# One region of program order for the opening and the first pass of a gated MLP, and five moves within it

## The chip, the cores and the metric

The kernel runs on one core of a Trainium2 chip. Its engines work side by side and meet through semaphores: TensorE (PE, with the load of its stationary operand listed apart as PEld), VectorE (DVE), ScalarE (ACT), GpSimd (POOL) and SyncE (SP), which issues all transfers. Each engine takes its instructions from a queue in order. The metric is the device time of one execution in microseconds. Before the change the median of 3 runs is 545.57 us (545.38 to 546.04).

## The reference

x is 2048 x 1024, w_gate and w_up are 1024 x 3584, w_down is 3584 x 1024, all bf16:

```python
g = jnp.einsum("bsd,df->bsf", x, w_gate)
u = jnp.einsum("bsd,df->bsf", x, w_up)
h = gelu(g) * u                      # tanh form
return jnp.einsum("bsf,fd->bsd", h, w_down)
```

## The kernel before

**Products by Winograd's scheme.** A matrix product split 2 x 2 needs eight half-size products; the kernel uses the form with seven, at the price of sums of operands. For the first two products the halves are: the two groups of 512 rows of x (c = 0, 1), the two halves of the 1024 input columns (k < 4 and k >= 4 in steps of 128), and a pair of 128-wide blocks of the weights. The sums of x are called T1 to T4, those of the weights S1 to S4 (`sums_t`, L148, `sums_s`, L163); TB and SA are plain casts of one quarter each to the type that PE wants. The T sums are made once by VectorE. The S sums are made by GpSimd for each pair of weight blocks while PE works on the pair before; only the first set is made by VectorE. The casts TB and SA are made by ScalarE.

**Passes and units.** There are two passes (`ip`) over 1024 rows each. A pass has 14 units (`unit`, L221), each for two of the 28 weight blocks, gate and up; then `down` multiplies the 1024 rows of h by w_down with the same scheme. A unit has 40 matmuls in five pairs of four: (S2, T2) accumulated onto the block's first product P1 in the banks e; (S1, T1) into the banks d; (S3, T3) onto e; (S4, TB) onto d; (SA, T4) onto e. Between them ScalarE copies e away as U2 (L108, before S3's product comes on top) and d as P5 (before S4's product comes on top), VectorE adds and multiplies, and ScalarE makes the gelus (L193). Gate and up have a bank each, so each of these steps is two instructions. In the first pass the copies U2 and P5 go to spare memory of the second half of x (`spare0`, listed as xT).

**Opening.** The first eight blocks are treated apart, as blocks 0 to 7 of plain products (`early_p1`, `early_p2`, L515 to L527): their first product P1 = (first half of x's columns) x (first half of the weights' rows) is copied away (`early_snap`, one of gate and up into a place of hT, the other into a slot p), the second product is added, and `early_c11` (L534) makes a gelu and a multiplication of the sum. These blocks' saved P1 come back later: unit u (u < 8) takes block u as its first and block u + 8 as its second block, and needs block u's P1 in its banks e. `seed` (L537) is the put-back, two copies by ScalarE. Unit 0's is made in the opening, that of unit u + 1 at the end of unit u (`ahead_of_p4`), in front of the fifth pair of products.

Before the first products, x's first 512 rows are turned by PE against an identity (`turn`, L456, four quarters) and copied out of PSUM; the other 512 rows are turned on their way in by SyncE's transposing transfers (L485), whose second half carries the operand of T2's and TB's inputs.

**Preparing w_down.** From unit 2 on the first pass also makes, for one 128-row block j of w_down per unit, three differences m for the last product (`keep_part`, L271): ScalarE casts a piece of the raw block into an idle PSUM bank (L277), VectorE subtracts. The first cast stands before U2 (`keep(0, ...)`), the second and third behind it. Then SyncE stores the differences (`store_made`, L287, 768 KB) and behind that fetches the raw block of the next unit (`fetch_wd`, L258, two loads of 256 KB, L269).

**Order.** SP, DVE, POOL and PE issue in the order of the source throughout. ScalarE does so only inside two kinds of region: one around the opening (L541), one around the units of each pass (L612). Within a region ScalarE keeps the order of the source; how the instructions of two regions fall between one another is left to the scheduler. `down` lies outside. Buffers of 2 KB per partition come from a pool of 52 slots (`slot`, L83), reused as they come free; weights have three larger ones.

Of the kernel before, what the change touches and what calls it, by code (L numbers as in the profile page):

```python
# [10 lines left out]
def kernel(  # L11
# [24 lines left out]
    ENG = mybir.EngineType  # L36
# [23 lines left out]
    R = 8  # L60
# [26 lines left out]
    bank = [psum.tile([P, N], f32, name=f"bank{i}") for i in range(8)]  # L87
# [18 lines left out]
    def snap(ps, name, at=None):  # L106
        t = slot([P, N], f32, name) if at is None else at
        nc.scalar.copy(out=t, in_=ps)  # L108
        return t
# [76 lines left out]
    def make_s(w, eng):  # L186
        s = sums_s(w, eng)
        s.make("s1", "s2", "s3", "sa", "s4")
        return s
# [28 lines left out]
        g, up = add(c, p1)  # L218
        times(fb, 0, gelu(g), up)

    def unit(fbs, banks, s, t, spare, after_p5, aside, keep, ahead_of_p4, behind_p4):  # L221
        GU = range(2)
        e, c, d = banks
        for i in GU:
            product(e[i], s["s2"][i], t["t2"], False)
        aside()
        keep(0, c[0])
        u2 = [snap(e[i], "u2", spare[i]) for i in GU]
        keep(1, c[0])
        keep(2, c[1])  # L230
        up = c[1]
        c = d
        for i in GU:
            product(c[i], s["s1"][i], t["t1"], True)
        p5 = [snap(c[i], "p5", spare[2 + i]) for i in GU]
        after_p5()
        for i in GU:
            product(e[i], s["s3"][i], t["t3"], False)
        g = new(dve, e[0], p5[0], ADD, "sum", dtype=f32)
        dve(up, e[1], p5[1], ADD)  # L240
        for i in GU:
            product(c[i], s["s4"][i], t["tb"], False)
        times(fbs[1], 1, gelu(g), up)
        g, up = add(c, u2)
        times(fbs[0], 1, gelu(g), up)
        ahead_of_p4()
        for i in GU:
            product(e[i], s["sa"][i], t["t4"], False)
        behind_p4()
        times(fbs[1], 0, gelu(e[0]), e[1])  # L250
# [108 lines left out]
    sa = {}  # L359
# [96 lines left out]
    def turn(ps, half, a, parts):  # L456
        tp = ps.bitcast(bf16).rearrange("p (k r) -> p k r", k=KH)
        for t in range(2):
            for k in range(KH):
                nc.tensor.transpose(  # L460
                    tp[:, k, t * P : (t + 1) * P], xn[half, a][:, t, k * P : (k + 1) * P], ident
                )
        n = KH // len(parts)
        for m, put in enumerate(parts):
            ks = slice(m * n, (m + 1) * n)
            put(  # L466
                out=xT[0][:, half * KH : (half + 1) * KH, a * 2 * P : (a + 1) * 2 * P][:, ks],
                in_=tp[:, ks],
            )
# [35 lines left out]
    def early(u):  # L505
        if u // 2 not in pairs_of:
            pairs_of[u // 2] = load_w((R + u) // 2, new_w())
        return [first[u], block_of(pairs_of[u // 2], u % 2)]
# [25 lines left out]
    def early_c11(u, ps):  # L534
        times(block(0, u, 0), 0, gelu(ps[0]), ps[1])

    def seed(u, e):  # L537
        for i in range(2):
            nc.scalar.copy(out=e[i], in_=p1s[u][i])

    with tc.manual_schedule(engines={ENG.Activation}):  # L541
        for _ in range(NWARM):
            nc.tensor.matmul(bank[3], lhsT=warm[:, :P], rhs=warm, start=True, stop=True)
        turn(bank[4], 0, 0, (on_dve,))
        turn(bank[5], 0, 1, (on_dve, on_act))
        pairs = [(u, ps, i) for u, ps in ((0, E), (1, K)) for i in range(2)]
        for cols in (slice(0, 2 * P), slice(2 * P, N)):
            for u, ps, i in pairs:
                early_p1(u, ps, i, range(0, 2), cols)
        for u, ps, i in pairs[:2]:  # L550
            early_p1(u, ps, i, range(2, KH))
        early_snap(0, E)
        turn(bank[6], 1, 0, (on_dve,))
        early_p1(*pairs[2], range(2, KH))
        turn(bank[7], 1, 1, (on_dve,))
        early_p1(*pairs[3], range(2, KH))
        early_snap(1, K)
        for ks in (range(0, 2), range(2, KH)):
            for u, ps, i in pairs:
                early_p2(u, ps, i, ks)  # L560
        early_c11(0, E)
        early_c11(1, K)
        four = ((2, C), (3, F), (4, E), (5, K))
        for u, ps in four:
            for i in range(2):
                early_p1(u, ps, i, range(KH))
            early_snap(u, ps)
        t.make("t1", "t2")
        for u, ps in four:
            for i in range(2):  # L570
                early_p2(u, ps, i, range(KH))
            early_c11(u, ps)
            if u == 3:
                t.make("t3")
            if u == 4:
                t.make("t4")
        seed(0, F)
        two = ((6, E), (7, K))
        for u, ps in two:
            for i in range(2):  # L580
                early_p1(u, ps, i, range(KH))
            early_snap(u, ps)
        t.make("tb")
        s.make("s1", "s2")
        pool_behind(s["s2"][-1][:, 0])
        s.make("s3", "s4", "sa")
        for u, ps in two:
            for i in range(2):
                early_p2(u, ps, i, range(KH))
            early_c11(u, ps)  # L590
        nxt = {"s": make_s(early(1), pool)}
    spare0 = [as_f32(xT[1][:, 2 * m : 2 * m + 2]) for m in range(4)]

    def making(u):
        if u < 2 or u >= NU:
            return []
        return list(range(u - 2, NJ if u == NU - 1 else u - 1))
# [13 lines left out]
    for ip in range(NPASS):  # L611
        with tc.manual_schedule(engines={ENG.Activation}):  # L612
            if ip == 0:
                ws = {}
            else:
                raw_of(0, F)()
                raw_of(1, C)()
            for u in range(NU):
                js = making(u) if ip == 0 else []

                def prepare():
                    if "s" not in nxt and u + 1 < NU:
                        nxt["s"] = make_s(weights(ip, u + 1), pool)
                    if len(js) == 1:
                        store_made(js[0])
                    for j in js[1:]:
                        keep_whole(j)
                    if ip == 0:
                        fetch_wd(making(u + 1))

                def keep(part, ps):
                    if js:
                        keep_part(js[0], part, ps)

                def aside():
                    if u + 2 < NU:
                        weights(ip, u + 2)

                def ahead_of_p4():
                    if u % 2 and u + 1 < NU and (ip or u + 1 >= R):  # L640
                        raw_of(u + 1, F)()
                        nxt["c11"] = raw_of(u + 2, C)

                    if ip == 0 and u + 1 < R:
                        seed(u + 1, F if u % 2 else C)

                def behind_p4():
                    if "c11" in nxt:
                        nxt.pop("c11")()

                if u % 2 and (ip or u):
                    E, K, C = C, E, K
                banks = (E, K, C) if u % 2 else (F, K, E)
                unit(
                    [block(ip, u, h) for h in range(2)], banks, s, t,
                    [None] * 4 if ip else spare0,
                    prepare, aside, keep, ahead_of_p4, behind_p4,
                )
                s = nxt.pop("s", None)

        last = ip == NPASS - 1
        got, nxt = {}, {}

        def more(step):
            if last:
                return
            if step in (-1, 0, 2):
                store_made({-1: NJ - 3, 0: NJ - 2, 2: NJ - 1}[step])
            if step == 0:
                xT[:] = new_x()  # L670
            if step >= 24 and step % 2 == 0 and step // 2 - 12 < len(moves):
                c, ko = moves[step // 2 - 12]
                transposing(xT, c, ko, (2 * (ip + 1) + c) * N)
            if step == 50:
                ws.clear()
                loaded(0), loaded(1)
            if step == 58:
                got["s"] = make_s(loaded(0), dve)
            if step == 62:
                got["t"] = make_t(xT)  # L680

        down(ip, F + K, C + E, last, more)
        E, K, C, F = K, E, F, C
        if not last:
            t, s = got["t"], got["s"]
# [29 lines left out]
```

## Time and profile before

| what | value |
|---|---|
| median of 3 runs | 545.57 us |
| the profiled execution: its time | 544.05 us |
| its span, first to last instruction | 542.3 us |
| PE busy | 534.3 us (99%) |
| DVE, ACT, POOL busy | 336.5, 273.3, 246.1 us |
| granted PE clock | 1.00 throughout |
| end of opening on PE, start of unit 0 | 36.0 us |
| start of units 1, 2, 3 on PE | 47.85, 57.10, 66.35 us |

A line of a timeline holds the start and the length in us from the span's start, the engine, the line of the kernel, the operation, what it writes and reads by the program's names, the shapes, how many instructions were merged, and in brackets how long the engine had been idle and what ended that. A line number may be that of a helper: L115 is every plain matmul, L91 every VectorE operation on two tensors, L94 the same of GpSimd, L103 a cast, L108 a copy out of PSUM, L193 a gelu, L539 a put-back of P1. "SPq" is SyncE's queue with its transfers. Matmuls are pipelined: starts are exact, ends modelled.

### The profile page before, as it was taken

What the parts mean: (1) busy time and instruction counts of PE and PEld (TensorE: products, weight loads), DVE (VectorE), ACT (ScalarE), POOL (GpSimd) and SP (SyncE); (2) the same over time, 40 slices, a digit from 0 to 9 for tenths busy, and PEclk for the clock granted to TensorE, in tenths of its full rate; (3) what the DMA queues carried; (4) which work ended last, traced back from release to release, by engine and by line L of the source; (5) the groups of instructions that cost most, each with busy time, mean ns of one, the idle gap of its engine ahead of it and who ended that gap; (6) DMA issues with size and microseconds to landing.
All of it is one profiled execution on the core that took longest, in us unless ns stands there. A gap on an engine that the chain in (4) does not pass through costs nothing.

```text
span 542.3 us, 7464 instructions
## 1 busy us (share of the span) xinstructions
PE 534.3 (99%) x2399; PEld 383.2 (71%) x2399; DVE 336.5 (62%) x516; ACT 273.3 (50%) x487; POOL 246.1 (45%) x221
## 2 busy tenths in 40 slices
PE   8979999999999999999999999999999999999997
PEld 4438787868676745888868676776768685488885
DVE  1675777667676795594964564555554639676730
ACT  4566787857666410166346555555555551114431
POOL 0049999986873500000076767676766600000000
PEclk9999999999999999999999999999999999999999
DMA  8943366956481999989854222232521049563751
GB/s 241 260 119 111 105 181 190 250 175 216 134 255 50 355 388 342 249 213 253 302 158 114 77 79 77 79 105 58 145 59 24 0 136 390 192 233 97 232 186 50
DMA packets 106471, 93.29 MB, mean 172 GB/s; under 512 B 17088, under 2 KB 91840, under 8 KB 106432
## 3 DMA queue, kind: packets, MB, share of 16 engines
q1 hardware_dynamic: 106432, 92.82, 58.1%
q8 instruction: 19, 0.31, 0.2%
q14 instruction: 20, 0.16, 0.1%
HBM read 74.45 MB, written 15.20 MB: 165 GB/s over the span
## 4 chain that ended last, share of the span: by engine, by line
PE 93%; SPq 3%; DVE 2%; DMA 1%; ACT 1%; issue 0%; DVEq 0%
PE bank L115 93%; DVE t L91 1%; DMA xT<-in_x_dram 1%; SPq L127 1%; SPq L485 1%; DVE hT L91 0%; SPq L449 0%; ACT sa L103 0%; ACT xT L108 0%; ACT st L418 0%; ACT g L193 0%; DVEq L91 0%
## 5 line engine op out<-in xcount | busy, mean ns | idle before, releaser
L94 POOL TENSOR_TENSOR s<-w 128x512 fp32r<-128x512 bf16 x92 | 106.5, 1177 | 138.2 <-PE bank L115 100.5
L115 PE MATMUL bank<-t,s 128*128 128x512 f32 x672 | 158.4, 391 | 2.2 <-ACT g L193 2.2
L115 PEld LDWEIGHTS bank<-t,s 128*128 128x128 f32 x672 | 125.5, 188 | 30.8 <-ACT g L193 2.6
L91 DVE TENSOR_TENSOR hT<-g,bank 128x512 bf16<-128x512 f32 x112 | 76.9, 688 | 26.0 <-ACT g L193 15.4
L193 ACT ACTIVATE g<-sum 128x512 f32<-128x512 f32 x76 | 48.2, 634 | 70.1 <-DVE sum L91 66.9
L115 PE MATMUL bank<-xT,w 128*128 128x512 bf16 (+1 forms) x360 | 78.6, 375 | 0.7 <-DVE xT L466 0.7
L108 ACT COPY p<-bank 128x512 f32<-128x512 f32 x92 | 52.7, 589 | 45.3 <-PE bank L115 45.3
L91 DVE TENSOR_TENSOR sum<-bank,p 128x512 f32<-128x512 f32 x34 | 23.5, 692 | 75.9 <-PE bank L115 75.9
L115 PEld LDWEIGHTS <-w 128*128 128x128 bf16 x360 | 34.1, 98 | 41.7 <-issue 2.6
L115 PE MATMUL bank<-q 128*128 128x512 f32 x240 | 58.9, 389 | 0.0
L115 PEld LDWEIGHTS <-hT 128*128 128x128 bf16 x320 | 31.1, 98 | 38.9 <-issue 1.7
L115 PE MATMUL bank<-t,sa 128*128 128x512 f32 x224 | 57.2, 397 | 0.0
L115 PE MATMUL bank<-tb,s 128*128 128x512 f32 x224 | 55.3, 389 | 0.0
L115 PEld LDWEIGHTS bank<-q 128*128 128x128 f32 x240 | 45.1, 188 | 9.3
L103 ACT CAST tb<-raw 128x512 fp32r<-128x512 bf16 x28 | 17.3, 627 | 62.9 <-PE bank L115 29.9
L115 PEld LDWEIGHTS bank<-t,sa 128*128 128x128 f32 x224 | 42.1, 188 | 9.5
L115 PE MATMUL bank<-raw,hT 128*128 128x512 bf16 x224 | 48.7, 379 | 0.0
L115 PEld LDWEIGHTS bank<-tb,s 128*128 128x128 f32 x224 | 42.1, 188 | 8.7
L94 POOL TENSOR_TENSOR s<-w,s 128x512 fp32r<-128x512 bf16 x40 | 46.0, 1171 | 0.0
L94 POOL TENSOR_TENSOR s<-s,w 128x512 fp32r<-128x512 f32 x40 | 45.7, 1163 | 0.0
L91 DVE TENSOR_TENSOR q<-hT 128x512 fp32r<-128x512 bf16 x56 | 38.4, 686 | 3.6 <-PE bank L115 3.4
L108 ACT COPY xT<-bank 128x512 f32<-128x512 f32 x56 | 31.7, 590 | 10.2 <-PE bank L115 8.6
(54 smaller groups left out, 568.1 us busy)
## 6 DMA issues: line engine op xcount, KB each, us to landing
raw<-in_w_down_dram SPq DMA_DIRECT2D x76, 256.0 KB, 4.8
q<-td SPq DMA_DIRECT2D x60, 256.0 KB, 5.0
w<-in_w_gate_dram SPq DMA_DIRECT2D x24, 512.0 KB, 5.5
w<-in_w_up_dram SPq DMA_DIRECT2D x24, 512.0 KB, 6.6
td<-m SPq DMA_DIRECT2D x12, 768.0 KB, 4.5
w<-td SPq DMA_DIRECT2D x6, 1024.0 KB, 10.1
out_dram<-st SPq DMA_DIRECT2D x32, 128.0 KB, 1.8
hT<-in_w_gate_dram SPq DMA_DIRECT2D x3, 512.0 KB, 5.0
```

The lines of the kernel that those rows point to most:

```text
L91: nc.vector.tensor_tensor(out=out, in0=a, in1=b, op=op)
L94: nc.gpsimd.tensor_tensor(out=out, in0=a, in1=b, op=op)
L103: nc.scalar.copy(out=t, in_=src)
L108: nc.scalar.copy(out=t, in_=ps)
L115: nc.tensor.matmul(ps, lhsT=lhs, rhs=rhs, start=start, stop=stop, skip_group_check=True)
L127: nc.sync.dma_start(out=w[:, i, k0:k1], in_=src[k0 * P : k1 * P, f0 : f0 + wide * P].rearrange("(ko ki) f -> ki ko f", ki=P),)
L193: nc.scalar.activation(g, src, ACT.Gelu_apprx_tanh)
L485: nc.sync.dma_start_transpose(out=xT[1][:, half * KH : (half + 1) * KH], in_=x2[N : 2 * N, half * N : (half + 1) * N],)
```

## The change

- The opening becomes a function, `opening()`, called inside the first pass's region, so that ScalarE has one region of source order for both.
- The copy of the last turned quarter of x is split into two halves on VectorE.
- The four casts TB are made behind block 2's gelu instead of behind the copies of block 7's P1.
- T4 is made behind block 5's multiplication instead of behind block 4's.
- The two casts SA of unit 0 are made behind the last two early gelus instead of in front of them in the source.
- The put-back for unit u + 1 is made right behind U2 of unit u, not in front of its fifth pair of products.

```diff
-    def unit(fbs, banks, s, t, spare, after_p5, aside, keep, ahead_of_p4, behind_p4):
+    def unit(fbs, banks, s, t, spare, behind_u2, after_p5, aside, keep, ahead_of_p4, behind_p4):
...
         u2 = [snap(e[i], "u2", spare[i]) for i in GU]
+        behind_u2()
         keep(1, c[0])
         keep(2, c[1])
...
-    with tc.manual_schedule(engines={ENG.Activation}):
+    def opening():
...
-        turn(bank[7], 1, 1, (on_dve,))
+        turn(bank[7], 1, 1, (on_dve, on_dve))
...
             early_c11(u, ps)
+            if u == 2:
+                t.make("tb")
             if u == 3:
                 t.make("t3")
-            if u == 4:
-                t.make("t4")
+        t.make("t4")
         seed(0, F)
...
-        t.make("tb")
         s.make("s1", "s2")
         pool_behind(s["s2"][-1][:, 0])
-        s.make("s3", "s4", "sa")
+        s.make("s3", "s4")
         for u, ps in two:
             for i in range(2):
                 early_p2(u, ps, i, range(KH))
             early_c11(u, ps)
-        nxt = {"s": make_s(early(1), pool)}
+        s.make("sa")
+        return {"s": make_s(early(1), pool)}
...
             if ip == 0:
                 ws = {}
+                nxt = opening()
...
+                def behind_u2():
+                    if ip == 0 and u + 1 < R:
+                        seed(u + 1, F if u % 2 else C)
...
-                    if ip == 0 and u + 1 < R:
-                        seed(u + 1, F if u % 2 else C)
```

More of the change, by code (lines that the diff above doesn't have):

```diff
@@ L656 @@
                     [None] * 4 if ip else spare0,
-                    prepare, aside, keep, ahead_of_p4, behind_p4,
+                    behind_u2, prepare, aside, keep, ahead_of_p4, behind_p4,
                 )
```

## The prediction

> **What bounds the kernel now.** The page's first part comes first: TensorE (PE) is busy 99% of the span, every other engine at most 62%.
>
> ```profile
> PE 534.3 (99%) x2399; PEld 383.2 (71%) x2399; DVE 336.5 (62%) x516; ACT 273.3 (50%) x487; POOL 246.1 (45%) x221
> ```
>
> So an edit can win only where PE stands still or starts a product late. The timeline of PE alone names two such places in the first 45 us, both in the stretch that the change reorders:
>
> ```profile
> 31.89 4.48 PE L115 MATMUL bank<-xT,hT 128*128 128x512 bf16 x20 [0.88 <-DVE hT L91]
> 36.02 2.21 PE L115 MATMUL bank<-t,s 128*128 128x512 f32 x8
> 40.44 3.92 PE L115 MATMUL bank<-t,s 128*128 128x512 f32 x16 [2.21 <-ACT g L193]
> ```
>
> The 2.21 us is the wait of unit 0's second pair of products for the gelus of blocks 6 and 7. ScalarE's timeline shows why. The first half of block 6's sums is complete after 8 of the 20 matmuls from 31.89 on (0.216 apart, the last 0.38 long: 33.8), that of block 7 after 16 (35.5); but the two gelus (L193) stand behind unit 0's copies of U2 (L108) and two casts, although the source writes them first.
>
> ```profile
> 37.34 0.59 ACT L108 COPY xT<-bank 128x512 f32<-128x512 f32 x1 [1.72 <-PE bank L115]
> 38.27 0.59 ACT L108 COPY xT<-bank 128x512 f32<-128x512 f32 x1 [0.34 <-PE bank L115]
> 38.75 1.14 ACT L103 CAST sa<-w 128x512 fp32r<-128x512 bf16 x2
> 39.79 1.09 ACT L193 ACTIVATE g<-bank 128x512 f32<-128x512 f32 x2
> ```
>
> A third loss is spread out. All engines' timeline at a unit boundary (unit 3 starts at 66.35):
>
> ```profile
> 65.63 0.58 ACT L539 COPY bank<-hT 128x512 f32<-128x512 f32 x1
> 66.15 0.58 ACT L539 COPY bank<-p 128x512 f32<-128x512 f32 x1
> 66.32 0.76 PEld L115 LDWEIGHTS bank<-t,s 128*128 128x128 f32 x4 [0.31 <-POOL s L94]
> 66.35 0.94 PE L115 MATMUL bank<-t,s 128*128 128x512 f32 x3
> ```
>
> The seed copy (L539) into the first bank ends at 66.21; the weight load, 0.31 idle, starts 0.11 later (its releaser is listed as POOL, long done; it was the seed). In units 1 to 7 PE starts 0.14 after that copy each time. Last, what can bind once PE is sooner: ScalarE, VectorE and SyncE around unit 3 and 4.
>
> ```profile
> 69.64 1.49 DVE L91 TENSOR_TENSOR m<-bank,m 128x512 fp32r<-128x512 f32 x2 [1.06 <-ACT bank L277]
> ```
> ```profile
> 71.15 0.33 SPq L288 DMA_DIRECT2D td<-m  x1
> 71.57 1.33 SPq L269 DMA_DIRECT2D raw<-in_w_down_dram  x2
> ```
> ```profile
> 76.42 0.59 ACT L277 CAST bank<-raw 128x512 f32<-128x512 bf16 x1
> 76.93 0.59 ACT L108 COPY xT<-bank 128x512 f32<-128x512 f32 x1
> ```
>
> Read as a ring: the third difference m ends at 71.13, its store and then the raw loads of the next block are issued, the first raw lands 4.8 us after its issue (76.38), and ScalarE's first cast of unit 4 starts 0.04 later. This ring turns in 9.25 us, the length of a unit; PE is not held by it yet.
>
> **The change part by part.** Times are in the profiled execution (span 542.3, its own time 544.05); the median of the runs shown is 545.57, 1.5 more, and a saving is taken to be the same in both.
>
> *Copy of the last turned quarter in two halves.* PE waits 0.44 us until 11.00 for a 0.69 us copy begun at 10.16. A 128x512 copy out of PSUM took 0.42 (at 5.42), so the first half is there at 10.58 and PE could start 0.28 earlier. Its third matmul needs weights that land at 11.13 (issued 5.33, 5.8 us to landing). Between 0 and 0.28 I take 0.15. The extra instruction costs VectorE 0.15, in 3 us of idle time.
>
> *The four TB casts moved up, behind the gelu of block 2.* Their 0.52 us steps (2.18 for four) now stand before the gelu of block 3: gelu 2 at 22.27, casts to 24.94, gelu 3 at 24.84 for 24.14. The operand landed at 22.04, so they don't wait. VectorE multiplies block 3 at 25.48 for 25.15, and everything behind is 0.33 later: T3, product of block 4 ending 29.16 for 28.84.
>
> *T4 behind the multiplication of block 5.* That one now ends at 29.76 instead of 31.84. PE: the second half of block 6's first product writes the bank that block 4's multiplication reads; it starts at 29.21 instead of a free 28.97 (0.24 lost). The second half of block 7's starts at 30.94 instead of 31.89. The 0.88 wait is gone, 0.95 is gained so far. VectorE goes on to T4, until 32.17, to S2, until 34.58, and S4, until 36.99; PE needs S2 at 35.25, T4 not before 42. GpSimd's set for unit 1 starts 0.33 later (34.64) and has its S2 at 41.5; unit 1 starts at 44.4. Its sets take 9.02 us each, so it stays 3 us ahead. On SyncE's queue nothing changes place here: the weights of these units are issued by 28 us, before and after.
>
> *Gelus 6 and 7 before U2.* Gelu 6 can run at 32.85, gelu 7 at 34.6. Unit 0's second pair then waits for the first multiplication behind S4 (37.59), and for its own turn: 35.25 + 1.86 = 37.11 for the first bank, 38.03 for the second, 0.3 after it is free. That pair's start moves from 40.44 to 37.11; and the first matmul after the stall, 0.34 before the second one, falls back to 0.23. So 3.44 up to here. The casts of SA moved between (four, 2.1) push the U2 copies to 37.17 and 37.65, seeds to 38.14, P5 to 39.17 and 39.65: needed at 38.95, 39.85, 40.78 and 41.69. If the covering slack of 0.3 on the multiplication fails, the loss is what it is late; bounds 0 and 0.9, I take 0.
>
> *Seeds behind U2.* PE's undisturbed step in this stretch is 0.2267 us (second half of every unit), so 40 matmuls take 9.07. Units 1 to 6 start on PE at 47.85, 57.10, 66.35, 75.62, 84.89, 94.14, the seventh at 103.41: 55.56 for 54.41. With the ends, seven boundaries cost 1.29. The seeds now run 6 us earlier; nothing else ends last there (S2 is 3 us early). Between 0 and 1.29 I take all of it.
>
> *What the seeds are moved in front of.* Two copies at 0.517 us now stand between U2 and the second and third cast of the w_down differences (L277), from unit 2 to unit 6. Behind them wait the differences on VectorE, their store, and on SyncE's queue behind the store the raw loads of the next block; and the P5 copies, which free the bank of PE's fourth pair. With K the start of the first cast, T the unit's start, and ScalarE never idle, from the steps of the rows (cast 0.52, copy 0.49, seeds 0.48 and 0.52, casts 0.52 and 0.52, P5 0.52 + 0.59): the second cast is at K + 2.52, P5's first copy ends at K + 4.15, the third difference at K + 2.52 + 2.12 (69.01 to 71.13) = K + 4.64. The fourth pair wants P5 at T + 5.44, 0.14 ahead as with the seeds: PE is held when K > T + 1.15, by that excess and 0.12 of restart. From the end of the third difference to the next first cast the five rows have 4.82, 5.26, 4.81, 5.29, 5.27 (more where two weight loads follow), and 0.04. So the ring needs 9.5 or 9.95 us, against 9.07 for PE.
> Unit 2 has its raw early: K = T - 0.2; U2's second copy waits for PE until T + 2.06, so P5 is out at T + 5.21 (0.1 to spare, no stall) and the third difference at T + 5.69. Unit 3: K = T + 5.69 + 4.82 + 0.04 - 9.07 = T + 1.48, stall 0.45. Unit 4: K = T + 1.48 + 9.94 - 9.52 = T + 1.9, stall 0.9. Units 5 and 6 likewise 0.45 and 0.9. Unit 7 has no seed, so its P5 comes a microsecond sooner after K. Sum 2.7. Bounds: 0 if the raw loads come without the ring; upward, 0.8 more per landing gives 5.9.
>
> [...] The trace, whose stores of m take 3.9 to 5.5 us (median 4.5) to landing, decides for the long ring.
>
> Sum: -3.44 - 1.29 + 2.7 = -2.0, that is 542.0 in a profiled execution and **543.5** against the median. Later stages hold no idle PE and move along; the order on ScalarE from unit 8 on stays.
>
> **The rivals.** *Ring hidden (540.8).* If the raws land as early in the unit as now, all 4.7 us stay. For it: seeds leave the unit's end, which frees a buffer slot 6 us earlier. Against: VectorE's differences wait for L277 in 14 of 36 places, 15.9 us in all.
> *Ring a little longer (546).* The raw buffers are reused slots; where the first raw waits for the unit's first gelu (as the second raw at 62.80 does), its landing slips by some 0.6 in each of four units: 2.4 back, -2.0 + 2.4 = +0.4, no change that shows.
> *Slower (548).* The first raw waits for the unit's second gelu, as the very first raws do (issue held at 47.16 by an ACT gelu, landed 49.84, 2.7 later). That gelu ends 8.2 after K, the ring becomes 10.9, and units 3 to 6 stall 1.2 + 3 x 1.8, unit 7 0.7: -4.7 + 7.3 = +2.6. It decides from 0.8 us more per landing than the rows have.
> *The order isn't what costs.* If ScalarE's gelus were late for their inputs, nothing would move (545.6). Against: the gelu at 39.79 shows no wait at all.
>
> **How the numbers follow.** Computed ring 0.50 (its own range 542.3 to 544.4); hidden ring 0.15; a little longer, or no effect, 0.17; slower 0.18. A measurement of this kernel tells 0.2% (1.1 us) from no change. Faster 0.65, same 0.17, slower 0.18. The range starts at the hidden ring with the whole 0.28 of the split copy (540.7), takes in the longer ring at 546 and goes 0.8 into the way to the slower case: 546.8, which leaves out most of that case and little else.
>
> **What would show it.** Right: no idle PE before unit 0's second pair (about 37.1); units 1 and 2 of 9.07 us; PE waiting for ACT xT (P5) by 0.4 to 0.9 before the fourth pair (tb) of units 3 to 6; the first cast of these units 1.4 to 2 us after the unit's start, behind its raw load. Wrong: units 3 to 6 of 9.07 us (hidden), or of 10 to 11 us (slower); PE idle by hT L91 near 38 us; any PE wait after unit 8, for which I see no reason.

## The result, and the profile after

| | before | after |
|---|---|---|
| median of 6 runs each, us | 545.48 (544.79 to 546.04) | 542.84 (542.59 to 544.01) |
| the profiled execution: its time, us | 544.05 | 542.84 |
| its span, us | 542.27 | 541.03 |
| start of unit 1 on PE, us | 47.85 | 44.15 |
| start of unit 8 on PE, us | 119.55 | 118.30 |
| from unit 8 to the end, us | 422.72 | 422.73 |

The changed kernel takes 0.9958 of the time before (95% interval 0.9945 to 0.9972): faster, by 2.64 us between the medians. Between the two profiled executions it is only 1.24 us of span. Both figures matter below.

The page after, the busy times and the group of the fourth pair of products:

```profile
PE 534.3 (99%) x2399; PEld 383.6 (71%) x2399; DVE 335.4 (62%) x517; ACT 272.3 (50%) x487; POOL 246.3 (46%) x221
...
L115 PE MATMUL bank<-tb,s 128*128 128x512 f32 x224 | 55.7, 391 | 2.3 <-ACT xT L108 2.3
```

PE's busy time is what it was; the split copy shows as one instruction more on VectorE. New is the idle time in front of the fourth pair, ended by P5's copy on ScalarE (line numbers are one or so higher than before). First the opening, PE's timeline after:

```profile
14.09 21.11 PE L115 MATMUL bank<-xT,hT 128*128 128x512 bf16 x96
34.84 5.84 PE L115 MATMUL bank<-t,s 128*128 128x512 f32 x24
```

The 96 matmuls of the early blocks are in one piece, but for 0.23 us lost at 28.99 (see below), and so are unit 0's first three pairs: neither the 0.88 us wait in front of block 7's second half nor the 2.21 us in front of unit 0's second pair is left. ScalarE's timeline shows the gelus of blocks 6 and 7 ahead of the casts and copies:

```profile
32.64 0.60 ACT L193 ACTIVATE g<-bank 128x512 f32<-128x512 f32 x1 [0.28 <-PE bank L115]
34.37 0.60 ACT L193 ACTIVATE g<-bank 128x512 f32<-128x512 f32 x1 [1.13 <-PE bank L115]
34.86 2.17 ACT L103 CAST sa<-w 128x512 fp32r<-128x512 bf16 x4
36.93 1.07 ACT L108 COPY xT<-bank 128x512 f32<-128x512 f32 x2
```

Then the first units, PE's timeline again:

```profile
62.30 5.60 PE L115 MATMUL bank<-t,s 128*128 128x512 f32 x24
68.06 2.08 PE L115 MATMUL bank<-tb,s 128*128 128x512 f32 x8 [0.16 <-ACT xT L108]
...
77.97 2.06 PE L115 MATMUL bank<-tb,s 128*128 128x512 f32 x8 [0.56 <-ACT xT L108]
...
88.56 2.06 PE L115 MATMUL bank<-tb,s 128*128 128x512 f32 x8 [0.96 <-ACT xT L108]
...
98.53 2.08 PE L115 MATMUL bank<-tb,s 128*128 128x512 f32 x8 [0.65 <-ACT xT L108]
```

Units 3, 4, 5 and 6 each wait for P5. ScalarE's timeline gives the reason: the first cast of the raw w_down block waits for its load each time, and the casts, put-backs (L540) and copies queued behind it slip with it.

```profile
63.76 0.59 ACT L278 CAST bank<-raw 128x512 f32<-128x512 bf16 x1 [0.75 <-DMA raw<-in_w_down_dram]
...
73.67 0.59 ACT L278 CAST bank<-raw 128x512 f32<-128x512 bf16 x1 [1.23 <-DMA raw<-in_w_down_dram]
...
84.27 0.59 ACT L278 CAST bank<-raw 128x512 f32<-128x512 bf16 x1 [1.85 <-DMA raw<-in_w_down_dram]
84.79 1.07 ACT L108 COPY xT<-bank 128x512 f32<-128x512 f32 x2
85.75 0.60 ACT L540 COPY bank<-hT 128x512 f32<-128x512 f32 x1
86.27 0.60 ACT L540 COPY bank<-p 128x512 f32<-128x512 f32 x1
86.79 1.12 ACT L278 CAST bank<-raw 128x512 f32<-128x512 bf16 x2
87.83 1.08 ACT L108 COPY xT<-bank 128x512 f32<-128x512 f32 x2
...
94.23 0.59 ACT L278 CAST bank<-raw 128x512 f32<-128x512 bf16 x1 [1.28 <-DMA raw<-in_w_down_dram]
```

In unit 5 (it starts at 81.68) ScalarE stands idle for 1.85 us until the raw block lands; the first P5 copy then ends near 88.4, and PE starts its fourth pair at 88.56 after its longest wait. A bracket counts from the modelled end of the matmul before; counted from start to start, a wait loses some 0.2 to 0.3 us more, so that the 2.3 us of the page stand for a larger loss in the next table.

The start of each unit on PE, taken from the matmuls' starts, in us, and the length of the unit:

| unit | before, start | length | after, start | length | first cast after the start |
|---|---|---|---|---|---|
| 0 | 36.02 | 11.82 | 34.84 | 9.30 | |
| 1 | 47.85 | 9.25 | 44.15 | 9.07 | |
| 2 | 57.10 | 9.25 | 53.22 | 9.09 | -0.18 |
| 3 | 66.35 | 9.27 | 62.30 | 9.51 | 1.46 |
| 4 | 75.62 | 9.27 | 71.81 | 9.87 | 1.86 |
| 5 | 84.89 | 9.25 | 81.68 | 10.60 | 2.59 |
| 6 | 94.14 | 9.27 | 92.28 | 10.00 | 1.95 |
| 7 | 103.41 | 16.14 | 102.28 | 16.02 | 1.88 |

So the account between the two profiles is: 3.70 us gained up to unit 1, 2.46 us given back from unit 1 to unit 8 (74.16 for 71.70), nothing behind. Of the 3.70, some 0.36 lies ahead of block 2's first product (14.09 for 14.45): about 0.17 of it is the split copy. From the last matmul ahead of that copy's wait to block 2's first product pass 4.11 us for 4.28 (4.01 to 4.21 in the five profiles on record with the split, 4.27 to 4.28 in the five without). The other 0.19 lies ahead of that and is not the change's: block 2's first product starts between 14.09 and 14.98 over all ten profiles, in no order of kernels.

### The profile page after: what moved, and what is told of

Same layout as the page of the kernel before. It is cut to its first block, busy times and chain, and to the rows that moved or that the text cites. A ratio compares the mean times of both kernels' runs of the same rounds, so it can differ in the third digit from the quotient of the medians.

```text
span 541.0 us, 7444 instructions
## 1 busy us (share of the span) xinstructions
PE 534.3 (99%) x2399; PEld 383.6 (71%) x2399; DVE 335.4 (62%) x517; ACT 272.3 (50%) x487; POOL 246.3 (46%) x221
## 4 chain that ended last, share of the span: by engine, by line
PE 94%; ACT 3%; DMA 1%; DVE 1%; issue 1%; SPq 0%; ACTq 0%; DVEq 0%
PE bank L115 93%; DMA raw<-in_w_down_dram 1%; ACT xT L108 1%; ACT bank L540 1%; ACT bank L278 1%; PE bank L544 1%; PE bank L461 0%; DVE t L91 0%; ACT tb L103 0%; DVE m L91 0%; DVE hT L91 0%; ACT g L193 0%; ACT st L419 0%; DVE xT L467 0%; SPq L289 0%
```

## The experiments

The theory at this point: the opening and the boundaries gain what was computed, and the put-back behind U2 lengthens the ring (first cast, U2, put-back, two casts, differences, store, raw load, next first cast) beyond a unit. Rivals: ScalarE simply has too much in front of P5, whatever the raw load does; or the profile of before hides something, since it lies 1.4 us below the median of its own runs.

### The put-back behind P5 instead of behind U2

```diff
         u2 = [snap(e[i], "u2", spare[i]) for i in GU]
-        behind_u2()
         keep(1, c[0])
...
         p5 = [snap(c[i], "p5", spare[2 + i]) for i in GU]
+        behind_u2()
         after_p5()
```

> The changed kernel with one move: the put-back of unit u + 1 stands behind the copies of P5, not in front of the second and third cast of the w_down differences. Theory (ring): cast, U2, put-back, casts, differences, store, raw load, next cast took 9.5 to 10.6 us in units 3 to 6 of the changed kernel against 9.07 of PE; without the 1.03 us of put-back in it, it takes 8.5 to 9 and is hidden. All eight boundaries keep their gain. Units 1 to 6 are 9.07 us each, the 3.7 us of stalls of units 3 to 6 are gone: 539.1 us. Rival (the late raw loads have another cause, such as slower transfers now that everything starts 3 us earlier): the first cast still starts 1.5 to 2.6 us into units 3 to 6, P5 1.0 sooner; about 0.4 of 3.7 stays only where it starts 2.2 or later: 539.1 to 539.6, but with the late casts visible.

Measured: 539.87 us (539.30 to 540.09) beside 545.83 for the kernel before, ratio 0.9889 (0.9874 to 0.9904); 0.8 more than expected, but 3.0 below the change. PE's timeline, the same stretch as above:

```profile
62.50 5.60 PE L115 MATMUL bank<-t,s 128*128 128x512 f32 x24
67.94 1.98 PE L115 MATMUL bank<-tb,s 128*128 128x512 f32 x8
69.75 1.98 PE L115 MATMUL bank<-t,sa 128*128 128x512 f32 x8
71.57 5.60 PE L115 MATMUL bank<-t,s 128*128 128x512 f32 x24
```

and ScalarE's:

```profile
63.13 0.59 ACT L278 CAST bank<-raw 128x512 f32<-128x512 bf16 x1
...
66.08 1.08 ACT L108 COPY xT<-bank 128x512 f32<-128x512 f32 x2
67.04 0.61 ACT L540 COPY bank<-hT 128x512 f32<-128x512 f32 x1
```

No bracket is left on either: units 1 to 6 take 9.07 us, the first cast comes 0.44 to 0.89 us into units 2 to 7 and finds its raw block there. From unit 1 to unit 8 it is 70.41 us. Against the 71.70 of before that is 1.29, the boundaries' whole gain; against the 74.16 of the change it is 3.7, the ring's whole cost.

### The raw loads ahead of the store

Here the put-back stays behind U2, and the only thing that changes is what stands in front of the raw loads on SyncE's queue.

```diff
+                    if ip == 0:
+                        fetch_wd(making(u + 1))
                     if len(js) == 1:
                         store_made(js[0])
                     for j in js[1:]:
                         keep_whole(j)
-                    if ip == 0:
-                        fetch_wd(making(u + 1))
```

> The changed kernel with one move on SyncE's queue: the raw loads of the next unit are issued ahead of the store of the differences. The put-backs stay where the change put them, in front of the casts and P5. Theory (ring): the raw loads no longer wait for the third difference and for the 768 KB in front of them; the first cast is not held by its data, P5 has 0.1 us to spare in every unit, the stalls of units 3 to 6 go: 539.1 us, at most 0.3 more. Rival (ScalarE is simply too full between U2 and P5, whatever its first cast waits for): the waits of the fourth pair for P5 stay at 0.3 to 1.1 us in units 3 to 6, and the time at 542.8.

Measured: 539.56 us (539.17 to 540.01), ratio 0.9885 (0.9870 to 0.9900). SyncE's queue and ScalarE's timeline of this kernel:

```profile
62.12 0.80 SPq L270 DMA_DIRECT2D raw<-in_w_down_dram  x2
68.55 0.33 SPq L289 DMA_DIRECT2D td<-m  x1
```
```profile
63.44 0.59 ACT L278 CAST bank<-raw 128x512 f32<-128x512 bf16 x1
...
65.37 0.60 ACT L540 COPY bank<-hT 128x512 f32<-128x512 f32 x1
65.89 0.59 ACT L540 COPY bank<-p 128x512 f32<-128x512 f32 x1
66.41 1.11 ACT L278 CAST bank<-raw 128x512 f32<-128x512 bf16 x2
```

The raw loads now go out 6.4 us ahead of the store. The put-backs still stand in front of the casts and of P5, and yet the units are 9.07 to 9.11 us long, with the first cast 0.52 to 0.61 us into units 3 to 7. That ScalarE has too much in front of P5 is thereby out: opening the ring at the transfer is enough. (Its opening lost 0.45 us more than the change's at block 6's first product. The second half of x landed later there, at 22.68 instead of 21.96 us, so T2 started 8.60 us behind block 2's first product instead of 7.97, and the multiplications that VectorE makes behind it came later too.)

### The put-back at the unit's end again, the rest of the change kept

```diff
         u2 = [snap(e[i], "u2", spare[i]) for i in GU]
-        behind_u2()
...
         ahead_of_p4()
+        behind_u2()
```

> The changed kernel with the put-back at the unit's end again, as before the change; all of the new opening stays. Theory: the gain of the opening alone, 3.4 us, without the gain of the boundaries (1.3) and without the ring (3.7): units 1 to 6 are 9.25 us again, 540.4 us. So moving the put-back cost the change 2.4 us net. Rival (the boundary wait has nothing to do with the put-back): the same as in the changed kernel without the ring, 539.1, units of 9.07.

Measured: 540.78 us (540.39 to 541.21), ratio 0.9908 (0.9893 to 0.9923). The boundary between units 3 and 4, all engines' timeline:

```profile
71.99 0.58 ACT L540 COPY bank<-p 128x512 f32<-128x512 f32 x1
72.17 0.30 PEld L115 LDWEIGHTS bank<-t,s 128*128 128x128 f32 x2 [0.31 <-POOL s L94]
72.20 0.47 PE L115 MATMUL bank<-t,s 128*128 128x512 f32 x1
```

The 0.31 us of the weight load are back, units last 9.25 to 9.27, and 71.71 us pass from unit 1 to unit 8 as before the change. So the moved put-back made the change 542.84 - 540.78 = 2.1 us slower than it is without that step (2.4 by the traces from unit 1 to unit 8), and the opening's part is worth more than the whole change brought.

### The put-back alone, in the kernel before

```diff
         u2 = [snap(e[i], "u2", spare[i]) for i in GU]
+        behind_u2()
         keep(1, c[0])
...
+                def behind_u2():
                     if ip == 0 and u + 1 < R:
                         seed(u + 1, F if u % 2 else C)
```

> The kernel before with the put-back moved behind U2 and nothing else. Theory: the boundaries give 1.3, the ring costs 2.7 to 3.7, the clock's drop stays: 545.8 + 1.4 to 2.4 = 547.2 to 548.2 us, slower than before. Rival (the ring binds only because the opening is 3.5 us shorter): no stall, 544.5 us.

Measured: 547.33 us (546.22 to 549.48, 12 runs) beside 545.92 (23 runs), ratio 1.0027 (1.0014 to 1.0041): slower, the only part of the change found to be so; the other parts were not each tried alone. Units 1 to 6 take 9.07, 9.09, 9.49, 9.89, 11.08 and 9.89 us, the pattern of the change with a worse unit 5. ScalarE's timeline there (the unit starts at 86.16):

```profile
89.19 0.59 ACT L278 CAST bank<-raw 128x512 f32<-128x512 bf16 x1 [2.31 <-DMA raw<-in_w_down_dram]
```

The store of unit 4's differences took 5.75 us to landing in this execution. So the ring doesn't need the shorter opening to bind. (The medians mix executions with and without a drop of the clock, which the next two experiments deal with: 5 of these 12 have it and 17 of the 23. Like with like, the put-back costs 1.8 us without the drop, 546.60 for 544.80, and 1.5 with it, 547.87 for 546.33.)

### The kernel before, profiled a second time

No edit. The accounts by profiles (1.24 us) and by medians (2.64 us) don't agree.

> The kernel before, unchanged, profiled once more. The profile before took 544.05 us, below all of its six timed runs (544.79 to 546.04). If the 1.4 us sit in the opening, the start of unit 1 is later than 47.85 us and the units are again 9.25; if they sit in the ring of the raw loads, some of units 3 to 8 are longer than 9.3; if it is the start of the execution, the first product is later.

Measured: 546.2 us, span 544.4, 2.1 us more than the first profile of the same kernel. PE's timeline:

```profile
36.56 2.20 PE L115 MATMUL bank<-t,s 128*128 128x512 f32 x8
40.97 5.53 PE L115 MATMUL bank<-t,s 128*128 128x512 f32 x16 [2.21 <-ACT g L193]
46.34 1.99 PE L115 MATMUL bank<-tb,s 128*128 128x512 f32 x8
```

The same wait of 2.21 us, but the 16 matmuls behind it take 5.53 us where the first profile had 3.92. The stretches around it, with the columns start and end, length, busy time (and instructions) of PE, PEld, DVE, ACT and POOL, granted clock, DMA share and GB/s:

```profile
36.00:40.90 4.90, 2.76 (x13) 1.71 (x10) 1.20 (x2) 2.84 (x7) 4.90 (x5) 1.00 0.00 0
40.90:44.90 4.00, 3.94 (x10) 3.13 (x11) 1.29 (x2) 1.25 (x4) 4.00 (x4) 0.57 0.00 0
44.90:49.90 5.00, 5.00 (x23) 3.96 (x22) 3.79 (x6) 3.27 (x7) 5.00 (x6) 1.00 0.00 0
```

The granted clock is 0.57 on average behind the wait; in detail it is 0.5 from 41.09 on, for 3.41 us (1.71 us of clock, as 0.43 of the row's 4.00 us is 1.72), and 8 matmuls start 0.427 us apart instead of 0.227. Unit 0 lasts 13.43 us instead of 11.82: 1.6 us lost, of which the first profile shows nothing. That is most of the 2.1. The other 0.54 lies ahead of unit 0, which starts that much later: x's second half landed at 22.58 instead of 22.04 us, and PE's waits for the multiplications behind T2 were longer (1.12 us instead of 0.88 ahead of block 7's second half, and a new one of 0.19 at 29.43). Units 1 to 6 last 9.23 to 9.35 us: the ring is not the place.

### The wait filled with products of constants

If the idle time brings the clock down, filling it must bring the kernel before to 544, although it starts nothing sooner. Eight matmuls of constants go between unit 0's first and second pair; nothing reads their results.

```diff
         up = c[1]
+        if fbs[0] == 0 and spare[0] is not None:
+            for _ in range(8):
+                nc.tensor.matmul(C[0], lhsT=warm[:, :P], rhs=warm, start=True, stop=True)
         c = d
```

> The kernel before, with 8 matmuls of constants into an idle bank on PE between unit 0's first and second pair, where it stands still for 2.21 us; nothing reads them, nothing else is moved. [...] Theory (clock): in the second profile of the kernel before, PE's granted clock is 0.57 in the 4 us behind that wait and its steps are 0.427 instead of 0.227 us for 8 matmuls, 1.6 us; the kernel before has this in most of its executions (mean clock 0.996 to 0.997, 545.7 to 546.9 us) and not in some (1.0, 544.1 to 544.5). With the wait filled no execution has it: clock 0.999 or 1.0, 544.1 to 544.5 us, 1.5 below the kernel before. Rival (the clock's drop has nothing to do with this idle time): same times and clocks as the kernel before, 545.8.

Measured: 544.33 us (543.83 to 545.26, 12 runs) beside 545.92 (23 runs), ratio 0.9971 (0.9960 to 0.9983). PE's timeline:

```profile
35.80 2.19 PE L115 MATMUL bank<-t,s 128*128 128x512 f32 x8
37.84 1.92 PE L234 MATMUL bank<-const-bfloat16-1.0 128*128 128x512 bf16 x8
40.20 3.94 PE L115 MATMUL bank<-t,s 128*128 128x512 f32 x16 [0.45 <-ACT g L193]
```

Useless work made the kernel 1.6 us faster. The mean granted clock of the whole execution sorts the runs, with a small overlap in time: it is 0.999 or 1.0 in all 12 here. Of the 23 executions of the kernel before, it is 0.996 or 0.997 in 17 (545.52 to 547.4 us) and 0.999 or 1.0 in 6 (544.07, 544.18, 544.61, 544.99, 545.15 and 545.68). A clock of half for 3.41 of 544 us is 0.003 off the mean, which is this difference. The medians of the 17 and the 6 are 546.33 and 544.80, 1.5 apart. So the profile that the prediction was worked from was one of the less usual executions.

### One region alone

The kernel before with its opening called inside the first pass's region, and nothing moved.

```diff
-    with tc.manual_schedule(engines={ENG.Activation}):
+    def opening():
...
-        nxt = {"s": make_s(early(1), pool)}
+        return {"s": make_s(early(1), pool)}
...
             if ip == 0:
                 ws = {}
+                nxt = opening()
```

> The kernel before with the opening inside the first pass's region and nothing else moved. Theory: the two gelus come before U2, PE's second pair of unit 0 starts 2.4 sooner, its 2.21 us of idle time go and with them the drop of the clock; the 0.88 wait at 31 us stays, the units stay 9.25: 545.8 - 2.5 - 1.6 = 541.7 us. The rest of the new opening (quarter, TB, T4) is then worth the difference to the run with the put-back at the end, 0.9. Rival (source order alone hides nothing, the gain of the opening came from T4 and TB): 544.5 or more.

Measured: 541.97 us (541.70 to 542.73), ratio 0.9931 (0.9914 to 0.9948), mean clock 0.999 or 1.0 in all 6. PE's timeline:

```profile
32.04 4.48 PE L115 MATMUL bank<-xT,hT 128*128 128x512 bf16 x20 [0.92 <-DVE hT L91]
36.16 5.83 PE L115 MATMUL bank<-t,s 128*128 128x512 f32 x24
```

and ScalarE's:

```profile
35.66 1.14 ACT L103 CAST sa<-w 128x512 fp32r<-128x512 bf16 x2
36.70 1.08 ACT L193 ACTIVATE g<-bank 128x512 f32<-128x512 f32 x2
37.67 1.14 ACT L103 CAST sa<-w 128x512 fp32r<-128x512 bf16 x2
38.70 2.16 ACT L108 COPY xT<-bank 128x512 f32<-128x512 f32 x4
```

The wait for block 5's multiplication stays, the 2.21 us are gone, although two casts SA still stand in front of the gelus: it was the U2 copies ahead of them that mattered. This one edit is worth 3.95 us, more than the whole change; 2.35 of it shows between the profiled executions, the other 1.6 agrees with the clock's price. It also beats the changed kernel by 0.9. (The two were not timed side by side; the kernel before, which was timed beside each, had medians of 545.48 and 545.92.) The kernel with the put-back at the unit's end has all of the new opening and takes 540.78, so the four other moves of the opening are worth 1.2 together, of which 0.85 shows from block 2's first product to unit 1 (30.06 us for 30.92).

### TB behind block 5, on top of the put-back behind P5

In front of T4 the casts cannot delay block 3's gelu.

```diff
             early_c11(u, ps)
-            if u == 2:
-                t.make("tb")
             if u == 3:
                 t.make("t3")
+        t.make("tb")
         t.make("t4")
```

> The version with the put-back behind P5, and the TB casts behind block 5's gelu instead of block 2's. Theory: the wait of 0.23 us at 28.8 (block 6's first product for block 4's multiplication, late by the casts) goes, nothing else is late: 539.87 - 0.2 = 539.6 us, not to be told apart by time, but by the trace. Rival (casts now delay the copies of block 6's and 7's first products): a wait for ACT before their second products at 31 to 33 us, 539.9 or more.

Measured: 539.82 us (539.50 to 540.60), ratio 0.9893 (0.9874 to 0.9911). The short wait near 28.8 us is gone, a step of 0.09 near 32.05 comes in its place, and the way from block 2's first product to unit 1 is 29.93 us for 30.05. In time it isn't told from the kernel with the put-back behind P5. That kernel, this one and the one with the raw loads first are the fastest, some 1.1% below the kernel before and 0.55% below the change.

## Why the prediction was right, and where it was not

The forecast was 543.5 us and the measured median is 542.84, within the range, and faster. But that it comes out this near is luck: two errors of opposite sign, a ring 1.0 us too short and a clock's drop of some 1.5 us that the working doesn't have, largely cancel.

**What held.** From block 2's first product to unit 1 the profiles gain 3.34 us; without the split copy the steps came to 3.29. The parts are there one by one: no idle PE ahead of the second pair, the 0.88 gone, and a wait where the earlier TB casts were to cost 0.24 (matmuls at 28.55 and 28.99 instead of 0.216 apart, 0.23 lost). The split copy was put at 0.15 and gave about 0.17. The boundaries were put at 1.29 and gave 1.29, shown with the ring out of the way by the put-back behind P5. The ring's mechanism is the one computed, with the waits at the place named (fourth pair, released by P5, behind a first cast that waits for its raw block); the raw loads ahead of the store took the ring away and left ScalarE's order, and nothing else did that was tried except taking the put-back out of it. The rivals fall with this: the ring isn't hidden, the first raw load is issued 0.42 to 0.45 us behind the store in units 2 to 6, with no gelu to wait for in between, and the order did cost. One reading of the lines was wrong without harm: of what stood in front of gelus 6 and 7, the source has the U2 copies behind them but the two casts SA in front, and in the kernel with one region alone those casts stay in front and PE doesn't wait.

**The ring's size failed in one term.** Computed for units 3 to 6 were 0.45, 0.9, 0.45 and 0.9, in sum 2.7. Measured, as the excess over 9.07, are 0.44, 0.80, 1.53 and 0.93, in sum 3.7. The step that failed is "units 5 and 6 likewise": the landing between units 4 and 5 was taken as that of the row before (4.81 from the third difference to the raw). The five landings measured are 4.83, 5.25, 5.94, 5.30 and 5.26, where the rows had 4.82, 5.26, 4.81, 5.29 and 5.27: all but this one came out as taken. SyncE's queue after, and the view by source line for that one store:

```profile
78.34 0.34 SPq L289 DMA_DIRECT2D td<-m  x1
78.79 1.32 SPq L270 DMA_DIRECT2D raw<-in_w_down_dram  x2
```
```profile
DMA to landing us min/median/max: 5.3/5.3/5.3
```

In the profile of before it took 3.93. The raw block landed at 84.25, 5.9 after the store's issue, so the first cast came 2.59 us into unit 5 instead of some 1.4. That put even U2's copy late (0.21 lost by PE near 85.5) and P5's (1.12 lost). With the ring closed, the 1.13 us of the later landing reached PE almost whole, as 1.1 us of stall more than computed; in the second profile of the kernel before, the same store was as slow (5.31) and unit 5 lasted 9.35 us instead of 9.25. The bound upward (5.9 for the sum, from 0.8 more per landing) covers the sum of 3.7, though this one landing slipped by more than 0.8.

**The sentence "a saving is taken to be the same in both" failed.** The profiled execution of before lay 1.5 below the median, and the prediction carried that difference over as a constant. Most of it was a cost with a place: the half clock behind the 2.21 us wait, seen in place in one profile, and by a mean clock of 0.996 or 0.997 in 17 of 23 executions. The change removes the wait, and all six of its executions have a mean clock of 0.999 or 1.0, so the cost is gone from its median, and no sum from profile to profile can show it: computed -2.0, profiled -1.24, medians -2.64. With the ring at 3.7 the working gives -1.0; with the 1.5 (the medians with and without the drop) to 1.6 (the filled wait) of the clock -2.5 to -2.6, where the medians say -2.64. Agreement to a tenth is more than these runs can carry: the first profile, 544.05, is also the fastest of all executions at full clock, whose median was 544.80, and when x lands moves the opening by some tenths. The profile of before couldn't show the clock; what could have been asked is where a difference of 1.5 us to the kernel's own median lies.

**What stays open.** The store of unit 4's differences took 3.55, 3.57, 3.93, 3.93, 4.08, 4.10, 5.29, 5.31, 5.75 and 5.76 us to landing over the ten profiles; meanwhile the two stores before it and the two behind it keep within 0.2 us each, apart from one. What decides it was not tried. Nor is it settled why the clock drops in some executions and not in others behind the same wait: in 17 of 23 of the kernel before, but in 5 of 12 with the put-back alone, whose profile has the same 2.21 us and no drop.

## What to carry to other kernels

When a step moves ahead on an engine, look for a ring through it: add up its way round to its own next turn, transfers and their queue included, and compare that with the period of the bound engine; if it doesn't fit, open the ring at the transfer, or move the step behind the last thing that the ring and the bound engine wait for. Before working from one profile, ask how its time stands to the median of the runs: a constant difference can be a cost that this execution happened not to pay, and the granted clocks of the runs can tell whether it did, as the means of 0.996 or 0.997 for 0.999 or 1.0 here. A wait on TensorE may cost more than its length, as the 2.21 us here did in 17 of 23 executions (by 1.5 us between the medians with and without the drop, by 1.6 us in the profile that has it), and its removal is then worth more than one trace shows.

## What the runs showed of the hardware

An idle TensorE of 2.21 us was followed by 3.41 us at half the clock, at a price of 1.6 us (8 steps of 0.427 us instead of 0.227): seen in place in the one profile that has it, and by a mean clock of 0.996 or 0.997 instead of 0.999 or 1.0 in 17 of 23 executions (and in 5 of 12 of the kernel with the put-back alone). In the kernel with one region alone, whose longest idle time behind block 2's first product is 0.92 us, the mean clock stayed at 0.999 to 1.0 in all 6 runs; so it did in the kernel with the filled wait (0.45 us left of it) in all 12, and in the changed kernel (0.96 us) in all 6.

Behind 2.21 us the mean clock was lower in 17 of 23 executions, behind 0.96 us in none of 6; no idle time between them was tried by itself.

SyncE's 768 KB store of the same tile at the same place of the program varies between 3.55 and 5.76 us to landing from one execution to the next.
